# Retention in chunks of 64 tokens: scores and K^T V in quadrants of the array, values and state in one product

## The chip, the cores and the metric

The kernel runs on one core of a Trainium2 chip. The metric is the device time of the program in microseconds; the kernel before takes 776.05 us, the median of 3 runs (775.56 to 776.47). The profiled execution of it has a span of 773.3 us.

In the profile PE is TensorE's matmuls, PEld its weight loads, DVE VectorE, ACT ScalarE, POOL GpSimd, and SP SyncE, which here issues nearly all transfers (SPq is its queue of instructions).

## The reference

Retention for 8 sequences of 576 tokens with 8 heads of 64 dimensions, then a feed-forward block of 4608 tokens, 512 to 768 to 512, whose hidden value is the maximum of three products.

```python
def _attn_ref(q, k, v):                       # each (8, 8, 576, 64)
    scores = scale * np.matmul(q, k.transpose(0, 1, 3, 2))
    gamma = 1.0 - 2.0 ** (-5.0 - np.arange(H))
    rel = pos[:, None] - pos[None, :]
    Dmat = np.where(rel >= 0, gamma[:, None, None] ** rel[None, :, :], 0.0)
    return np.matmul(scores * Dmat[None], v)

def _moe_ref(x, w1, w2, w3, w_out):           # x is (4608, 512)
    h = np.maximum(np.maximum(x @ w1, x @ w2), x @ w3)
    return h @ w_out
```

Because the decay is a power of gamma, retention can be computed by chunks: inside a chunk with masked scores, and for all earlier tokens through a state, the sum of K^T V so far (64x64 for each head). Values are scaled with gamma to a negative power beforehand, outputs with gamma to a positive one afterwards, and the state is multiplied by gamma^128 from one group of 128 tokens to the next.

## The kernel before

All 4608 tokens are cut into 36 groups `g` of 128 tokens (`C = 128`), four to a tile of 512 tokens. A sequence has 4.5 groups, so every second one begins at token 64 of a group. While the feed-forward block of one tile runs, the groups of the next tile are prepared in 12 steps strewn among its products. The parts that matter here (cuts are marked with `...`):

```python
def load_blocks(g, *blocks):                   # q and k in blocks of 32x32, to be transposed by VectorE
    for n, src in (("q", q), ("kx", k)):
        if 0 in blocks:
            raws[n, g] = raw.tile([P, NP, C // 32, 32], FP32, tag=n, name=n + "raw", bufs=2)
        for blk in blocks:
            for a in range(4):
                nc.sync.dma_start(t[32 * a:32 * a + 32, :, blk, :], src[...])   # 4 heads x 32 x 32

def load(g):                                   # blocks of q and k, then k and v as they are
    if g >= BY_PE and ("q", g) not in raws:
        load_blocks(g, *range(C // 32))
    for n, src in ...:
        bufs = 3 if n == "k" else 2
        ...
            nc.sync.dma_start(t[row:row + m], src[b, :, pos:pos + m, :].rearrange("h p d -> p h d"))

def decay_values(g):
    t = vds[g] = vpool.tile([C, H, D], FP32, tag="vd", name="vd")
    nc.gpsimd.tensor_tensor(t[:], raws.pop(("v", g))[:], gk[:]..., op=ALU.mult)

def scores(g):                                 # two heads at a time, 64 rows of the array each
    chore(len(urgent))                         # first whatever was put off
    for p in range(NP):
        for j in range(2):
            r = slice(D * j, D * (j + 1))
            nc.tensor.matmul(s[j][:, p, :], lhsT=kT[r, p, :], rhs=qT[r, p, :], start=True, stop=True)
    for j in range(2):
        soon(partial(nc.vector.tensor_tensor, st[:, j], s[j][:], masks[start_of(g)][:]..., op=ALU.mult))

def state(g):                                  # K^T V
    for h in range(H):
        nc.tensor.matmul(kvs[g][half(h % 2), h // 2, :], lhsT=kr[r:, h, :], rhs=vds[g][r:, h, :], ...)

def values(chunks, new_states=(), later=False):
    chore(len(urgent))
    for m, g in enumerate(chunks):             # scores times values
        for n in range(NP):
            for c in range(2):
                nc.tensor.matmul(o[n % 2][half(c), m, n // 2, :], lhsT=vds[g][:, h, :], rhs=sts[g][:, h % 2, h // 2, :], ...)
    for g in new_states:
        if g not in kvs:
            state(g)                           # also that of the next pair's first group
    for m, g in enumerate(chunks):             # state times queries, added to it
        ...
                nc.tensor.matmul(o[n % 2][half(c), m, n // 2, :old], lhsT=states[g][r, h // 2, :],
                                 rhs=qks[g]["q"][r, h // 2, :old], start=False, stop=True, ...)

for n in range(0, CPT, 2):                     # the 12 steps of a tile: m is 0 or 6
    a, b, m = CPT * t + n, CPT * t + n + 1, 6 * (n // 2)
    at(m, (keep, a), (transposes, b), (decay_values, b))
    at(m, (load, b + 2))
    at(m + 2, (scores, a), (scores, b))
    at(m + 3, (decay_values, a + 2))
    at(m + 4, (values, [a, b], [b, a + 2]), (transposes, a + 2), (load, a + 4))
```

`soon` puts a step into a queue from which the program takes one at a time between products of the feed-forward block. Groups up to 6 are transposed by TensorE, later ones (`g >= BY_PE`) by VectorE in blocks of 32x32. Every fp32 matmul is two passes, and shows as two instructions in the profile.

Of the kernel before, what the change touches and what calls it, by code (L numbers as in the profile page):

```python
# [80 lines left out]
def kernel(  # L81
# [30 lines left out]
    stp = ctx.enter_context(tc.tile_pool(name="stp", bufs=4))  # L112
# [15 lines left out]
    gk = const.tile([C, H], FP32, name="gk")  # L128
    one, top, inf, first = (const.tile([P, 1], FP32, name=n) for n in ("one", "top", "inf", "first"))
    const.tile([P, FILL // 4], FP32, name="fill")  # L130
    gq = const.tile([P, 2, NP // 2, C], FP32, name="gq")
    gs = const.tile([P, NP, D], FP32, name="gs")
# [6 lines left out]
    causal = const.tile([C, C], FP32, name="causal")  # L139
    nc.gpsimd.memset(causal[:], 1.0)  # L140
    nc.gpsimd.affine_select(out=causal[:], in_=causal[:], compare_op=ALU.is_ge, fill=0.0,
                            base=0, channel_multiplier=-1, pattern=[[1, C]])
# [8 lines left out]
    def start_of(g):  # L151
        r = -g * C % S
        return r if r < C else None

    masks = {0: causal, None: causal}
    for r in sorted({start_of(g) for g in range(NG)} - {0, None}):
        m = masks[r] = const.tile([C, C], FP32, name=f"causal{r}")
        nc.gpsimd.tensor_copy(m[:], causal[:])
        nc.gpsimd.memset(m[0:r, r:C], 0.0)


    raws, vds, qks, sts, states, kvs = {}, {}, {}, {}, {}, {}

    def spans(g):

        row = 0
        while row < C:
            b, pos = divmod(g * C + row, S)
            n = min(C - row, S - pos)
            yield row, b, pos, n  # L170
            row += n

# [14 lines left out]
    def load_blocks(g, *blocks):  # L187
        for n, src in (("q", q), ("kx", k)):

            if 0 in blocks:  # L190
                raws[n, g] = raw.tile([P, NP, C // 32, 32], FP32, tag=n, name=n + "raw", bufs=2)
            t = raws[n, g]
            for blk in blocks:
                b, pos = divmod(g * C + 32 * blk, S)
                for a in range(4):
                    nc.sync.dma_start(
                        t[32 * a:32 * a + 32, :, blk, :],
                        src[b, a // 2::2, pos:pos + 32, 32 * (a % 2):32 * (a % 2) + 32].rearrange("p j i -> j p i"))
# [12 lines left out]

    def decay_values(g):
        t = vds[g] = vpool.tile([C, H, D], FP32, tag="vd", name="vd")
        nc.gpsimd.tensor_tensor(t[:], raws.pop(("v", g))[:], gk[:].unsqueeze(2).to_broadcast([C, H, D]),  # L214
                                op=ALU.mult)
# [4 lines left out]
    def transposes(g):  # L220
        both = qks[g] = {}
        if g >= BY_PE:
            for n in ("k", "q"):
                t = both[n] = att.tile([P, NP, C], FP32, tag=n + "T", name=n + "T", bufs=2 if n == "k" else 3)
                soon(partial(nc.vector.transpose, t[:].rearrange("a p c -> a (p c)"),
                             raws.pop(("kx" if n == "k" else n, g))[:].rearrange("a p b i -> a (p b i)")))
            return
        for n, src in (("k", raws["k", g]), ("q", raws.pop(("q", g)))):
            pool, tag = (ps_r, "r") if g >= CPT else (ps_x, "x")
            pt = pool.tile([P, NP, C], FP32, tag=tag, name=n + "t")  # L230
            for p in range(NP):
                nc.tensor.transpose(pt[:, p, :], pair(src, p), ident[:C, :C])
            t = both[n] = att.tile([P, NP, C], FP32, tag=n + "T", name=n + "T", bufs=2 if n == "k" else 3)
            nc.scalar.copy(t[:], pt[:])

    def scores(g):
        chore(len(urgent))
        qT, kT = qks[g]["q"], qks[g]["k"]
        s = [ps_r.tile([C, NP, C], FP32, tag="r", name=f"s{j}") for j in range(2)]
        for p in range(NP):  # L240
            for j in range(2):
                r = slice(D * j, D * (j + 1))
                nc.tensor.matmul(s[j][:, p, :], lhsT=kT[r, p, :], rhs=qT[r, p, :], start=True, stop=True)  # L243
        st = sts[g] = att.tile([C, 2, NP, C], FP32, tag="st", name="st", bufs=2)
        for j in range(2):
            soon(partial(nc.vector.tensor_tensor, st[:, j], s[j][:],
                         masks[start_of(g)][:].unsqueeze(1).to_broadcast([C, NP, C]), op=ALU.mult))

    def begins(g):
        return g + 1 < NG and start_of(g + 1) != 0  # L250

    def half(j):
        return slice(D * j, D * (j + 1))

    def state(g):

        kr = raws["k", g]
        kvs[g] = None
        if begins(g):
            r = start_of(g) or 0  # L260
            kvs[g] = ps_r.tile([P, NP, D], FP32, tag="r", name="kv")
            for h in range(H):
                nc.tensor.matmul(kvs[g][half(h % 2), h // 2, :], lhsT=kr[r:, h, :], rhs=vds[g][r:, h, :],  # L263
                                 start=True, stop=True)

    def keep(g):
        def step(t, kv):
            if start_of(g) is not None:
                nc.vector.tensor_tensor(t[:], kv[:], gs[:], op=ALU.mult)
            else:  # L270
                nc.vector.tensor_tensor(t[:], kv[:], states[g][:], op=ALU.add)  # L271
                nc.gpsimd.tensor_tensor(t[:], t[:], gs[:], op=ALU.mult)  # L272

        if begins(g):
            t = states[g + 1] = stp.tile([P, NP, D], FP32, tag="state", name="state")
            soon(partial(step, t, kvs[g]))
# [7 lines left out]
    def values(chunks, new_states=(), later=False):  # L284

        def before(g):
            return C if start_of(g) is None else start_of(g)

# [3 lines left out]
        o = [pool.tile([P, len(chunks), NP // 2, C], FP32, tag=tag, name="o") for _ in range(2)]  # L294
        for m, g in enumerate(chunks):
            for n in range(NP):
                for c in range(2):
                    h = head(c, n)
                    nc.tensor.matmul(o[n % 2][half(c), m, n // 2, :], lhsT=vds[g][:, h, :],  # L299
                                     rhs=sts[g][:, h % 2, h // 2, :], start=m == 0 and n < 2,  # L300
                                     stop=before(g) == 0, skip_group_check=True)
        for g in new_states:
            if g not in kvs:
                state(g)
        for m, g in enumerate(chunks):
            old = before(g)
            if old > 0:
                for n in range(NP):
                    for c in range(2):
                        h = head(c, n)  # L310
                        r = half(h % 2)
                        nc.tensor.matmul(o[n % 2][half(c), m, n // 2, :old], lhsT=states[g][r, h // 2, :],  # L312
                                         rhs=qks[g]["q"][r, h // 2, :old], start=False, stop=True,
                                         skip_group_check=True)
        finish = partial(output, chunks, o, t, i)
        if later:
            return finish
        finish()
        for g in new_states[:1]:
            if g >= CPT:  # L320
                keep(g)

    def output(chunks, o, t, i):
        if i == 0:
            xT[t] = xpool.tile([P, NDC, NT], FP32, tag="xT", name="xT")
        for b in range(2):
            shape = [P, NP // 2, len(chunks), C]
            soon(partial(
                nc.vector.tensor_tensor,
                xT[t][:, b::2, i * C:(i + len(chunks)) * C].rearrange("p u (m c) -> p u m c", c=C),  # L330
                o[b][:].rearrange("p m u c -> p u m c"), gq[:, b].unsqueeze(2).to_broadcast(shape), op=ALU.mult))
        i += len(chunks) - 1
# [285 lines left out]
    def ffn(t):  # L618

        h = hpool.tile([P, NF, NT], FP32, tag="h", name="h")  # L620
        if t == 0:
            for fp, i in units:
                for fb in (2 * fp, 2 * fp + 1):
                    maximum = up_plain(t, h, fb, i)
                    if CPT not in qks:
# [63 lines left out]
    for g in range(CPT):  # L689
        load(g)  # L690
        if g == 1:
            for j in range(2):
                nc.sync.dma_start(gs[half(j)], state_decay[half(j), :, half(j)])
# [5 lines left out]
    for c in range(2):  # L699
        of_rows = out_decay[:, NP // 2 * c:NP // 2 * (c + 1), :].rearrange("(b p) u c -> p b (u c)", b=2)  # L700
        nc.scalar.dma_start(gq[half(c)].rearrange("p b u c -> p b (u c)"), of_rows)
# [4 lines left out]
    state(0)  # L706
    first_output = values([0], [0], later=True)
    keep(0)
# [4 lines left out]
    state(1)  # L713
    keep(1)
    values([1], [1])
# [4 lines left out]
    state(2)  # L720
    keep(2)
    convert(2)
    values([2], [2])
    convert(2)
    values([3], [3])
    convert(4)
    keep(3)
# [3 lines left out]
    def steps(t):  # L731
# [4 lines left out]
        def at(n, *what):  # L736
            for step, *args in what:
                if step is values:
                    if args[0][0] < NG:
                        todo[n].append(partial(values, args[0], [g for g in args[1] if g < NG]))  # L740
                elif args[0] < NG:
                    todo[n].append(partial(soon, partial(step, *args)) if step is load else partial(step, *args))

        if t == 1:
            a, b, c, d = range(CPT, 2 * CPT)
            at(0, (load, b))
            at(1, (scores, a), (state, a), (keep, a))
# [3 lines left out]
            at(5, (values, [a, b], [b, c]), (load_blocks, d, 3), (load, d))  # L751
# [76 lines left out]
```

## Time and profile before

| what | value |
|---|---|
| time, median of 3 runs | 776.05 us |
| span of the profiled execution | 773.3 us |
| PE busy | 766.8 us (99%) |
| VectorE busy | 564.1 us (73%) |
| ScalarE busy | 325.9 us (42%) |
| GpSimd busy | 102.9 us (13%) |
| scores, L243 | 576 matmuls, 37.7 us busy |
| scores times values, L299 | 576 matmuls, 35.7 us |
| K^T V, L263 | 512 matmuls, 19.2 us |
| state times queries, L312 | 512 matmuls, 18.4 us |
| block loads of q and k | 464 + 464 transfers of 16 KB |

How to read it: "busy" is the time in which at least one instruction of the kind was under way, and matmuls overlap, so these sums say less than the time from the first matmul of a kind to the next one of another kind. The chain of waits follows the work that ended last back to the beginning; its shares say which engine sets the time. A form such as 64\*128 64x128 means 64 rows and 128 columns of the array in use, with 128 columns of the moving operand. Up to about 24.6 us the first four groups are prepared alone; until about 122 us the weights are converted and the first tile is computed plainly; from then on a tile takes about 82 us, and the last tile has no retention beside it.

### The profile page before, as it was taken

Reading aid. Unit: us, or ns where it says so; the run is one execution under the profiler, and the core shown is the slowest. Engines: PE = TensorE matmul, PEld = TensorE weight load, DVE = VectorE, ACT = ScalarE, POOL = GpSimd, SP = SyncE. Lnnn points to the kernel's source line nnn. Section 1 sums busy time; section 2 is a strip of 40 time slices with the busy share of each in tenths; the row PEclk is TensorE's granted clock in tenths of the full one; section 3 lists DMA queues with packets and bytes.
Section 4 is the critical chain, followed back from the end, with each engine's and each line's share of the span. In section 5 each row is a group of like instructions: output and inputs, shape, how many; then the busy total and the mean of one; then the engine's idle time right before and its main releaser. Section 6 shows DMA issues by size and latency. Waiting matters only on the chain.

```text
span 773.3 us, 14511 instructions
## 1 busy us (share of the span) xinstructions
PE 766.8 (99%) x5032; PEld 626.5 (81%) x5032; DVE 564.1 (73%) x1249; ACT 325.9 (42%) x811; POOL 102.9 (13%) x124
## 2 busy tenths in 40 slices
PE   9999999999999999999999999999999999999998
PEld 8545454688888888888888888888888888888887
DVE  3898989799577856784768757876778568845672
ACT  3665631163254415451346234532544054514551
POOL 2210021111110201111111111110112001200000
PEclk9999999999999999999999999999999999999999
DMA  9995544333333332333233333333333323001001
GB/s 225 241 226 131 158 110 103 59 58 58 92 58 58 57 77 62 56 75 67 62 56 58 59 96 58 57 58 96 58 56 59 84 48 74 3 15 42 2 1 55
DMA packets 237083, 59.33 MB, mean 77 GB/s; under 512 B 217937, under 2 KB 235729, under 8 KB 237009
## 3 DMA queue, kind: packets, MB, share of 16 engines
q1 hardware_dynamic: 236432, 58.07, 34.9%
q8 instruction: 39, 0.64, 0.3%
q10 hardware_dynamic: 576, 0.33, 0.1%
q14 instruction: 36, 0.29, 0.1%
HBM read 48.89 MB, written 9.44 MB: 75 GB/s over the span
## 4 chain that ended last, share of the span: by engine, by line
PE 97%; SPq 1%; DVE 1%; DMA 1%; issue 0%; ACT 0%; DVEq 0%
PE a L588 18%; PE b L588 16%; PE dx L428 11%; PE up L611 11%; PE c L588 8%; PE dz L428 5%; PE d L588 5%; PE e L588 5%; PE s L243 4%; PE o L299 4%; PE down L598 3%; PE dy L428 3%; PE o L312 2%; PE kv L263 2%; SPq L210 1%; DMA qraw<-in_q_dram 1%
## 5 line engine op out<-in xcount | busy, mean ns | idle before, releaser
L568 DVE TENSOR_TENSOR part<-part 128x256 f32<-128x256 f32 x460 | 208.7, 462 | 78.2 <-ACT part L573 70.4
L573 ACT COPY part<-b 128x256 f32<-128x256 f32 x230 | 85.6, 372 | 126.0 <-PE b L588 114.6
L573 ACT COPY part<-a 128x256 f32<-128x256 f32 x276 | 102.7, 372 | 84.9 <-PE a L588 72.3
L214 POOL TENSOR_TENSOR vd<-vraw,gk 128x512 f32<-128x512 f32 x36 | 40.3, 1120 | 339.2 <-DMA vraw<-in_v_dram 219.9
L611 PE MATMUL up<-xT,w 128*128 128x512 f32 (+2 forms) x200 | 84.7, 578 | 0.3 <-DVE w L517 0.3
L588 PE MATMUL a<-s,w 128*128 128x256 f32 x276 | 82.3, 380 | 0.0
L588 PE MATMUL b<-s,n 128*128 128x256 f32 x276 | 82.1, 379 | 0.0
L611 PEld LDWEIGHTS up<-xT,w 128*128 128x128 f32 x200 | 36.8, 190 | 42.3 <-issue 39.2
L588 PEld LDWEIGHTS b<-s,n 128*128 128x128 f32 x276 | 52.4, 190 | 7.1
L588 PEld LDWEIGHTS a<-s,w 128*128 128x128 f32 x276 | 52.3, 190 | 7.3 <-issue 0.2
L588 PE MATMUL c<-xT,w 128*128 128x256 f32 x184 | 56.0, 386 | 0.0
L588 PE MATMUL b<-xT,n 128*128 128x256 f32 x184 | 55.4, 382 | 0.0
L588 PE MATMUL d<-s,w 128*128 128x256 f32 x184 | 55.1, 381 | 0.0
L568 DVE TENSOR_TENSOR h<-part 128x256 f32<-128x256 f32 x92 | 42.6, 463 | 6.6
L588 PE MATMUL e<-xT,w 128*128 128x256 f32 x184 | 47.3, 379 | 0.0
L588 PE MATMUL a<-xT,n 128*128 128x256 f32 x184 | 47.2, 379 | 0.0
L428 PE MATMUL dx<-To,H 128*128 128x256 f32 (+1 forms) x204 | 44.9, 370 | 0.0
L435 ACT COPY part<-dx 128x256 f32<-128x256 f32 (+1 forms) x34 | 10.5, 363 | 80.1 <-PE dx L428 77.9
L178 DVE TENSOR_TENSOR xT<-o,gq 128x512 f32<-128x512 f32 x28 | 18.1, 686 | 33.3 <-PE o L312 33.3
L428 PEld LDWEIGHTS dx<-To,H 128*128 128x128 f32 x204 | 36.6, 190 | 5.5 <-issue 1.0
L243 PEld LDWEIGHTS s<-qT,kT 64*128 64x128 f32 x576 | 33.9, 188 | 7.9 <-PE b L588 4.0
L272 POOL TENSOR_TENSOR state<-state,gs 128x256 f32<-128x256 f32 x24 | 18.6, 776 | 162.1 <-DVE state L271 162.1
(104 smaller groups left out, 1299.8 us busy)
## 6 DMA issues: line engine op xcount, KB each, us to landing
bits<-in_moe_w_dram SPq DMA_DIRECT2D x36, 256.0 KB, 5.6
out_dram<-osb SPq DMA_DIRECT2D x35, 256.0 KB, 2.1
kraw<-in_k_dram SPq DMA_DIRECT2D x32, 256.0 KB, 3.0
vraw<-in_v_dram SPq DMA_DIRECT2D x32, 256.0 KB, 3.4
qraw<-in_q_dram SPq DMA_DIRECT2D x464, 16.0 KB, 1.8
kxraw<-in_k_dram SPq DMA_DIRECT2D x464, 16.0 KB, 1.8
bits<-in_moe_w_out_dram SPq DMA_DIRECT2D x6, 512.0 KB, 4.7
qraw<-in_q_dram SPq DMA_DIRECT2D x6, 256.0 KB, 4.1
```

What stands on the lines that cost most here:

```text
L178: (urgent or chores).popleft()()
L214: nc.gpsimd.tensor_tensor(t[:], raws.pop(("v", g))[:], gk[:].unsqueeze(2).to_broadcast([C, H, D]), op=ALU.mult)
L243: nc.tensor.matmul(s[j][:, p, :], lhsT=kT[r, p, :], rhs=qT[r, p, :], start=True, stop=True)
L263: nc.tensor.matmul(kvs[g][half(h % 2), h // 2, :], lhsT=kr[r:, h, :], rhs=vds[g][r:, h, :], start=True, stop=True)
L272: nc.gpsimd.tensor_tensor(t[:], t[:], gs[:], op=ALU.mult)
L299: nc.tensor.matmul(o[n % 2][half(c), m, n // 2, :], lhsT=vds[g][:, h, :], rhs=sts[g][:, h % 2, h // 2, :], start=m == 0 and n < 2, stop=be ...
L428: nc.tensor.matmul(o, lhsT=hS[n](fp)[:, m * P:(m + 1) * P], rhs=late["T"][n][:, fp, cols], start=first and fp == 0 and (m == 0 or last and ...
L568: nc.vector.tensor_tensor(out, a, b, op=op)
L573: nc.scalar.copy(t[:], ps[step[0]][:])
L588: nc.tensor.matmul(ps[chain][:], lhsT=factor(w, fb), rhs=xS[t][x], start=n == 1, stop=ends, skip_group_check=True)
L598: nc.tensor.matmul(b[:], lhsT=h[:, fb, m * P:(m + 1) * P], rhs=w_sb["out", fb], start=(fb == 0), stop=(fb == NF - 1))
L611: nc.tensor.matmul(ps[:, cols], lhsT=w_sb[i, fb][:, dc * P:(dc + 1) * P], rhs=xT[t][:, dc, cols], start=dc == 0 and cols.start == 0, stop= ...
```

## The change

The unit becomes 64 tokens: each group has two chunks `c`. Scores (64x64 for a head) and K^T V of each chunk (contraction over 64 tokens) are laid out so that four matmuls use the four 64x64 quadrants of the array. The masked scores of a chunk and its queries are stacked in one 128-row operand `ms[g, c]`, its values and the state in another, `vas[g, c]`, so that one product over 128 rows gives values plus state times queries. It is meant to take matmul time off TensorE.

For the stacking the halves have to lie in fixed rows: chunk 0 has values in rows 0 to 63 and the state in rows 64 to 127, chunk 1 the reverse. Values and queries of chunk 0 are moved there by transfers within the core (`move_values`, `move_queries`); for groups up to 6 the scaling and the copies out of PSUM are split instead. Masks and additions of the state (`keep`) now write halves. The state of chunk 0 is added without a decay, and that of chunk 1 is multiplied by GpSimd. Block loads take eight heads at a time. The diff, cut to its core:

```diff
@@ load_blocks
-                raws[n, g] = raw.tile([P, NP, C // 32, 32], FP32, tag=n, name=n + "raw", bufs=2)
+                raws[n, g] = raw.tile([P, H, 2, 32], FP32, tag=n, name=n + "raw", bufs=2)
-                for a in range(4):
+                c, e = divmod(blk, 2)
+                for a in range(2):
+                    r = D * (1 - c) + 32 * a
                     nc.sync.dma_start(
-                        t[32 * a:32 * a + 32, :, blk, :], ...
+                        t[r:r + 32, :, e, :],
+                        src[b, :, pos:pos + 32, 32 * a:32 * a + 32].rearrange("h p i -> p h i"))
@@ values, scaled and moved
+        if g >= BY_PE:
+            vas[g, 1] = vpool.tile([P, H, D], FP32, tag="va1", name="va1")
+            scaled(vas[g, 1], slice(0, C))
+            return
+        for c in range(2):
+            scaled(fresh(g, c), half(c))
+
+    def move_values(g):
+        nc.sync.dma_start(fresh(g, 0)[half(0)], vas[g, 1][half(0)])
...
@@ transposes
-            t = both[n] = att.tile([P, NP, C], FP32, tag=n + "T", ...)
-            nc.scalar.copy(t[:], pt[:])
+            copy = nc.vector.tensor_copy if n == "q" and g < CPT else nc.scalar.copy
+            for c in range(2):
+                for j in range(2):
+                    copy(to[c][half(1 - c), j::2, :], pt[half(j), :, half(c)])
+
+    def move_queries(g):
+        def step():
+            m0 = ms[g, 0] = att.tile([P, H, D], FP32, tag="m0", name="m0", bufs=3)
+            nc.sync.dma_start(m0[half(1)], ms[g, 1][half(1)])
+        soon(step)
@@ scores, now with K^T V
-                nc.tensor.matmul(s[j][:, p, :], lhsT=kT[r, p, :], rhs=qT[r, p, :], start=True, stop=True)
+        for h in range(H):
+            for c in range(2):
+                if place(g, c) < S // D - 1:
+                    nc.tensor.matmul(sk[c][half(c), h, :], lhsT=kr[half(c), h, :], rhs=vas[g, c][half(c), h, :], ...)
+            for c in (1, 0):
+                r = half(1 - c)
+                nc.tensor.matmul(sk[1 - c][half(c), h, :], lhsT=kT[r, h, :], rhs=of_q[c][r, h, :], ...)
+
+        def mask(c):
+            nc.vector.tensor_tensor(ms[g, c][half(c)], sk[1 - c][half(c)], causal[half(c)]..., op=ALU.mult)
+
+        def keep(c):
+            to = fresh(g + 1, 0) if c else vas[g, 1]
+            if place(g, c) == 0:
+                nc.scalar.copy(to[half(c)], sk[c][half(c)])
+            else:
+                nc.vector.tensor_tensor(to[half(c)], sk[c][half(c)], vas[g, c][half(1 - c)], op=ALU.add)
+            if c:
+                nc.gpsimd.tensor_tensor(to[half(1)], to[half(1)], gs[half(1)]..., op=ALU.mult)
...
@@ values
+            for m in range(2):
+                for n in range(NP):
+                    for c in range(2):
+                        nc.tensor.matmul(o[half(c), n, half(m)], lhsT=vas[g, m][:, h, :], rhs=ms[g, m][:, h, :], ...)
...
@@ the steps of a tile
-            at(m, (keep, a), (transposes, b), (decay_values, b))
+            at(m, (move_queries, a), (transposes, b), (decay_values, b))
             at(m, (load, b + 2))
+            at(m + 1, (move_values, b), (move_queries, b))
             at(m + 2, (scores, a), (scores, b))
             at(m + 3, (decay_values, a + 2))
-            at(m + 4, (values, [a, b], [b, a + 2]), (transposes, a + 2), (load, a + 4))
+            at(m + 4, (values, a, b), (move_values, a + 2), (transposes, a + 2), (load, a + 4))
```

## The prediction

> **What bounds the kernel now.** I read, in this order, the page's busy times and its chain, the groups of matmuls, the tensor engine's order of time around one pair of groups, and the order of time of the queue that issues transfers (SPq). From the page and the first 24.6 us:
>
> ```profile
> PE   9999999999999999999999999999999999999998
> PEld 8545454688888888888888888888888888888887
> DVE  3898989799577856784768757876778568845672
> PE 97%; SPq 1%; DVE 1%; DMA 1%; issue 0%; ACT 0%; DVEq 0%
> 0.00:24.60 24.60, 20.98 (x288) 18.39 (x288) 11.78 (x26) 8.97 (x14) 7.68 (x16) 1.00 0.97 218
> 24.60:98.40 73.80, 73.79 (x352) 38.33 (x353) 68.44 (x125) 45.33 (x69) 7.45 (x7) 1.00 0.79 188
> ```
>
> PE is the bound: 97% of the chain, no gap after 24.6 us. VectorE (third pair of numbers) has 5 us to spare out of 74 in the stage in which the weights are converted. So a us taken from PE counts whole from 122.6 us on; every new wait of PE counts whole as well, since nothing else hides behind it.
>
> What retention costs on PE, from one pair of groups (start, length, engine, line, tiles; a piece lasts until the next one starts):
>
> ```profile
> 219.74 2.06 PE L243 MATMUL s<-qT,kT 64*128 64x128 f32 x32
> 221.72 0.70 PE L588 MATMUL c<-xT,w 128*128 128x256 f32 x2
> ...
> 273.57 1.97 PE L299 MATMUL o<-st,vd 128*64 128x128 f32 x32
> 275.37 1.10 PE L263 MATMUL kv<-vd,kraw 128*64 128x64 f32 x32
> 276.40 1.10 PE L312 MATMUL o<-qT,state 64*64 64x128 f32 x32
> 277.44 0.91 PE L428 MATMUL dx<-To,H 128*128 128x256 f32 x3
> ```
>
> A pair takes 1.98 (scores) + 1.80 (values) + 1.03 (K^T V) + 1.04 (state times queries) = 5.85 us. Over 122.6:700, where 14 pairs lie, the chain of waits gives the four lines 4.8 + 4.6 + 2.0 + 2.2 = 13.6% of 577.4 us, 78.5 us, or 5.6 a pair: first and last groups of a sequence need less.
>
> Does a quadrant with 64 moving columns cost half of one with 128? The kernel before has such matmuls, for groups in which a sequence begins at token 64:
>
> ```profile
> 66.95 0.90 PE L312 MATMUL o<-qT,state 64*64 64x64 f32 x32
> 67.78 7.13 PE L611 MATMUL up<-xT,w 128*128 128x512 f32 x16
> ```
>
> Half of these 32 move 64 columns, half 128: 0.83 us against the 1.04 of 32 wide ones. With 27.25 ns for a wide one (a 256-column matmul takes 216 ns, 2.59 us for twelve in the chain; half of that, shared by four quadrants, is 27) a fixed 0.16 is left of 1.03, and 0.83 = 0.16 + 16 x 27.25 + 16 x n gives n = 14.6 ns. So narrow quadrants do run four at a time.
>
> The queue that issues transfers (start, length, in order):
>
> ```profile
> 198.37 10.86 SPq L440 DMA_DIRECT2D out_dram<-osb  x4
> 209.32 7.57 SPq L196 DMA_DIRECT2D qraw<-in_q_dram  x16
> 216.94 8.68 SPq L196 DMA_DIRECT2D kxraw<-in_k_dram  x16
> 225.72 0.38 SPq L210 DMA_DIRECT2D kraw<-in_k_dram  x1
> 226.20 0.53 SPq L210 DMA_DIRECT2D vraw<-in_v_dram  x1
> 226.82 7.98 SPq L196 DMA_DIRECT2D qraw<-in_q_dram  x16
> ```
>
> This queue is seldom idle: the load of one group holds it for 17.5 us (209.32 to 226.82), two groups in the 41 us of a pair. A transfer costs it some 0.47 us (7.57/16) whether it has 16 KB or 256 KB (0.38, 0.53). Today that is harmless, because loads run two groups ahead.
>
> **What the Trainium skill says.** "TensorEngine Tiling", Key Properties: tiles load and multiply independently, but a change of tiling mode drains the array. The trace agrees: four quadrants share a 108 ns slot, and about 0.16 us is left over where the mode changes. The same page, PSUM Bottleneck: tiling speeds up TensorE and not the emptying of PSUM. It agrees: masking 128x512 takes VectorE 683 ns before, and 64 rows by 512 columns will, by my estimate, take as long. "DMA: Bandwidth & Descriptors", Anatomy of one DMA: a semaphore wait happens on the issuing sequencer, before dispatch. Our queue fits: the four stores sit on it for 10.86 us until their data is there. "TensorE: Matmul & The Clock Gate", Part 1: after an idle window of about 3.4 us the array runs at half its clock. The first transposes of the trace take 0.85 us for four (4.15 to 5.00), later ones 0.44 (28.18 to 28.62); no idle gap of that length lies later in this trace.
>
> **The change, part by part.**
> Matmuls of a pair. Scores and K^T V: 2 groups (of 128 tokens) x 8 heads x 4 quadrants x 2 passes = 128 x 14.6 ns + 0.16 = 2.03 us. Values with the state stacked: 2 x 8 x 2 x 2 = 64, two column tiles at a time, 29.2 ns each (kv before: 32 in 0.93 of its 1.03) + 0.1 = 1.97. Sum 4.0, 14 pairs 56.0. Saved: 78.5 - 56 = 22.5 us.
>
> VectorE. Of each group the state's addition (409 ns at 128x256) becomes two of 683 ns: about 1 us a group, 3 to 4 us in a tile of 82 us in which it is busy 58 to 60 us. Hidden in the steady part. At the start it isn't: the q copies of four groups move to VectorE as quarters, 16 x about 0.37 = 5.9 us, and 15 masks and additions instead of 8 masks and 3 additions give 10.2 against 6.7 us. Additions now stand ahead of each values product, with GpSimd's factors (two products of 1.04 us instead of one, and 1 us for the state) between them. With four outputs (2.7) and the first weight's conversion (2.9), VectorE's work before the first up product adds up to 21.7 us, from 6.1 us on, with some 3 us of waits: first up at about 30.8 instead of 24.61, +6 us.
>
> While the weights are converted PE would save 3.6 us, but VectorE, at 93%, gets 2.4 us more, and ScalarE copies 8 quarters (372 ns each for 256 columns) instead of 2 halves (590 ns): +1 us net.
>
> Transfers, the part that I think decides. Block loads are halved, 16 a group: 16 x 0.474 + 0.4 + 0.5 + some 0.5 of hiccups = 9.1 us. Two moves a group come in on the same queue, and PE waits for one: K^T V of a group's first half reads values that the queue must first have moved. For the second group of a pair, b, the code puts this move behind the whole load of group b+2. Take the tile that starts at 208.15 us (PE's previous dx ends there). The first scores start at +11.6, those of b at +12.6. On the queue the last store goes at +0.7; behind it stand the load of the group a+2 (9.1), the move of queries (0.5), the load of b+2 (9.1): the move of values goes at about +19.3, and lands some 2.3 us later (16 KB loads land after 1.8, 256 KB after 3.0). PE waits from +12.6 to +21.6: 9 us. In the second pair the queue is free, but the load of b+2 wants a buffer of kraw. There are three, and kraw is now read by the scores of group a, where the kernel before had read it one pair earlier. So: scores of a end, kraw 0.4, vraw 0.5, move 0.5, landing 2.3 with 512 KB ahead of it: about 4 us of PE's time.
>
> Groups 13 and 31 need no moved values for that product (their first half ends a sequence), 35 has no load in front: 6 waits of 9 us (54), 5 of 4 us (20), and for 13 and 31 a VectorE that waits for moved queries, 2 x 3. Each long wait lets the clock fall, an estimate of 1 to 2 us each, 8 in all.
>
> Sum: 776 - 22.5 + 6 + 1 + 54 + 20 + 6 + 8 = 848.5. Because all waits have been taken at full length, I go a little under: 842 us.
>
> **The rivals.**
> First, moves in time: transfers of eight heads take the queue less than 0.2 us each, or PE comes late anyway. Then 776 - 22.5 + 6 + 1 + 2 = about 762. For it: whoever put the moves a step ahead of the scores wanted that, and the number of loads was halved. Against it: no transfer in the lines above costs the queue under 0.38 us, and two loads stand before the move.
> Second, only the kraw wait is real, and the queue gets to the first pair early: 11 waits of 4 us, about 806.
> Third, VectorE becomes the bound in the steady part, as it empties PSUM of four more half tiles a pair: 62 of 78 us speak against it; it would add 5 to 10 us on top of any of these.
> Fourth, quadrants are issue-bound: starts 7 ns apart and 14.6 ns a matmul say no; it would leave the matmuls as long as before, +20.
>
> **Range and chances.** Four fifths of my belief lies with the queue, between the second rival (with shorter waits, 790) and full waits with a slow clock (875). The first rival gets the rest, shared between just over and just under 760.5 us, which is the 2% line. Range 788 to 872; faster 0.08, same 0.14, slower 0.78.
>
> **What would show it.** Quadrants: 128 matmuls of one pair in 2.0 us, net of waits. Waits: PE's waits led by a DMA of the moved values (va0<-va1), about eleven times, long (about 9) and short (about 4) in turn, always between the scores of a and of b; the queue's order of time with that move straight after kraw and vraw. Start: the first up near 30.8 us. Clock: matmuls of 256 columns at more than 216 ns after a long wait. I am wrong if PE is again without gaps after the start, or if the waits sit elsewhere, before the values product, say, on a mask or an addition.

## The result: 931.49 us, and the profile after

The changed kernel takes 931.49 us (median of 4 runs, 929.84 to 934.42) against 776.15 us: a ratio of 1.2006, with an interval of 1.1985 to 1.2027. That is 155 us slower; the prediction had 66 us and a range that ended at 872.

The page of the changed kernel, span 929.1 us: the busy rows in 40 slices, the granted clock in tenths, the chain by engine, and two of its groups and transfers (count, then KB and median us from issue to landing).

```profile
PE   7698999597996697796939697796949994999998
...
DVE  4879998396747666485528566585538763885672
...
PEclk8799999798997899798969899798969997999999
...
PE 62%; SPq 11%; DVE 11%; DMA 8%; issue 6%; ACT 2%; POOL 0%; DVEq 0%; ACTq 0%
...
L277 PE MATMUL sk<-va,kraw 64*64 64x64 f32 x1024 | 52.5, 254 | 118.8 <-DMA va<-va 82.4
...
va<-va SPq DMA_DIRECT2D x29, 128.0 KB, 3.2
```

PE, which before had nines to the end, has a hole about every second slice, and the clock row dips in the same places. The chain has left PE for 38% of the span, most of it for the issuing queue and transfers (SPq 11%, DMA 8%, issue 6%). One group of matmuls has nearly all of the idle time in front of it: K^T V, 118.8 us.

PE's waits of the changed kernel (us in all, times, longest) say the same by releaser:

```profile
PE sk L277 <- DMA va<-va: 82.4, 8, 14.5
PE sk L277 <- issue: 32.1, 3, 12.3
PE d L589 <- DVE part L569: 9.5, 1, 9.5
PE up L612 <- DVE w L518: 9.0, 2, 4.7
PE sk L277 <- POOL va L224: 4.3, 6, 0.8
```

The first two lines are eleven waits, 114.5 us, all before the scores of the second group of a pair. Three of them are put down to "issue", which is time for which the profile shows no cause; but they stand at the same place in the program and end at the same event. Here is one of those three, the pair of groups 16 and 17, with PE first and then the queue's order of time (start, length):

```profile
364.80 0.23 PE L281 MATMUL sk<-m,kT 64*64 64x64 f32 x2
377.00 0.33 PE L277 MATMUL sk<-va,kraw 64*64 64x64 f32 x1 [11.97 <-issue]
```

```profile
352.99 0.37 SPq L441 DMA_DIRECT2D out_dram<-osb  x1
353.45 3.92 SPq L195 DMA_DIRECT2D qraw<-in_q_dram  x8
357.41 3.90 SPq L195 DMA_DIRECT2D kxraw<-in_k_dram  x8
...
362.48 0.94 SPq L264 DMA_DIRECT2D m<-m  x1
363.52 4.01 SPq L195 DMA_DIRECT2D qraw<-in_q_dram  x8
367.58 3.92 SPq L195 DMA_DIRECT2D kxraw<-in_k_dram  x8
...
372.67 0.74 SPq L234 DMA_DIRECT2D va<-va  x1
...
374.15 0.54 SPq L234 DMA_DIRECT2D va<-va  x1
401.66 3.79 SPq L195 DMA_DIRECT2D qraw<-in_q_dram  x8
```

Two whole loads (353.45 and 363.52, nine us each) stand between the last store and the move of values that PE needs. The values themselves have been ready since 339.3, when GpSimd had scaled them. PE is ready for the move at 365.0; the queue issues it at 372.67, it lands at 376.9, and PE goes on at 377.00. The blocks of q and k that make up nearly all of those two loads are first read at 399.0, when VectorE transposes them.

The time from the first matmul to the next of another kind, without gaps, added up for three stretches (my own sums from the starts in each trace; "steady" is from the first product with sums of tiles to the end):

| us | first up product | from there to the steady part | steady: gaps | retention | other products | rest |
|---|---|---|---|---|---|---|
| before | 24.6 | 120.8 | 0 | 76.7 | 548.1 | 3.1 |
| after | 37.8 | 145.4 | 115.9 | 67.0 | 559.6 | 3.4 |
| difference | +13.2 | +24.6 | +115.9 | -9.7 | +11.5 | +0.3 |

The first of the eleven waits (11.5 us, at 173 us) lies in the second column.

### The profile page after: what moved, and what is told of

Its sections match the earlier page's. It is cut to its first block, busy times and chain, and to the rows that moved or that the text cites. A ratio compares the mean times of both kernels' runs of the same rounds, so it can differ in the third digit from the quotient of the medians.

```text
span 929.1 us, 16538 instructions
## 1 busy us (share of the span) xinstructions
PE 777.0 (84%) x6184; PEld 629.4 (68%) x6184; DVE 607.0 (65%) x1285; ACT 337.7 (36%) x845; POOL 131.4 (14%) x146
## 4 chain that ended last, share of the span: by engine, by line
PE 62%; SPq 11%; DVE 11%; DMA 8%; issue 6%; ACT 2%; POOL 0%; DVEq 0%; ACTq 0%
PE a L589 11%; PE b L589 10%; PE dx L429 9%; SPq L195 9%; PE c L589 6%; PE dz L429 4%; PE o L321 4%; PE d L589 4%; DMA va<-va 3%; DVE part L569 3%; PE e L589 3%; PE up L612 3%; PE sk L277 3%; PE down L599 2%; PE dy L429 2%
## 5 line engine op out<-in xcount | busy, mean ns | idle before, releaser
L277 PE MATMUL sk<-va,kraw 64*64 64x64 f32 x1024 | 52.5, 254 | 118.8 <-DMA va<-va 82.4
L277 PEld LDWEIGHTS sk<-va,kraw 64*64 64x64 f32 x1024 | 47.2, 164 | 128.4 <-issue 119.3
L294 DVE TENSOR_TENSOR va<-sk,va 64x512 f32<-64x512 f32 x56 | 38.6, 689 | 92.5 <-PE sk L281 89.0
L612 PE MATMUL up<-xT,w 128*128 128x512 f32 (+2 forms) x200 | 90.7, 611 | 9.1 <-DVE w L518 9.0
L296 POOL TENSOR_TENSOR va<-va,gs 64x512 f32<-64x512 f32 x32 | 35.3, 1107 | 410.1 <-DVE va L294 182.3
L285 DVE TENSOR_TENSOR m<-sk,causal 64x512 f32<-64x512 f32 x72 | 49.5, 687 | 19.9 <-DMA m<-m 15.4
L589 PE MATMUL c<-xT,w 128*128 128x256 f32 x184 | 61.5, 418 | 0.0
L224 POOL TENSOR_TENSOR va<-vraw,gk 128x512 f32<-128x512 f32 (+1 forms) x43 | 48.0, 1117 | 35.5 <-DMA vraw<-in_v_dram 27.2
L281 PE MATMUL sk<-m,kT 64*64 64x64 f32 x1152 | 50.7, 252 | 0.0
L281 PEld LDWEIGHTS sk<-m,kT 64*64 64x64 f32 x1152 | 45.6, 163 | 0.2 <-ACT m L258 0.2
```

The costliest lines, as they stand in the source:

```text
L224: nc.gpsimd.tensor_tensor(t[rows], v_raw[rows], factor, op=ALU.mult)
L277: nc.tensor.matmul(sk[c][half(c), h, :], lhsT=kr[half(c), h, :], rhs=vas[g, c][half(c), h, :], start=True, stop=True)
L281: nc.tensor.matmul(sk[1 - c][half(c), h, :], lhsT=kT[r, h, :], rhs=of_q[c][r, h, :], start=True, stop=True)
L285: nc.vector.tensor_tensor(ms[g, c][half(c)], sk[1 - c][half(c)], causal[half(c)].unsqueeze(1).to_broadcast([D, H, D]), op=ALU.mult)
L294: nc.vector.tensor_tensor(to[half(c)], sk[c][half(c)], vas[g, c][half(1 - c)], op=ALU.add)
L589: nc.tensor.matmul(ps[chain][:], lhsT=factor(w, fb), rhs=xS[t][x], start=n == 1, stop=ends, skip_group_check=True)
```

## The experiments

The theory: the moves wait behind loads on a queue that issues in order, and this makes up most of the loss. The rivals: the buffers of kraw (which I had taken for the cause in every second pair), the transfers themselves (their latency, whatever their place), and an overloaded VectorE. Ratios are to the kernel before, which took 776.4 to 776.7 us beside these runs.

**Moves ahead of the load.** The same transfers on the same queue, but values and queries of group b are moved before the load of b+2.

```diff
-            at(m, (move_queries, a), (transposes, b), (decay_values, b))
+            at(m, (move_queries, a), (transposes, b), (decay_values, b), (move_values, b), (move_queries, b))
             if a == 2 * CPT:
                 at(m, (load, a + 2))
             at(m, (load, b + 2))
-            at(m + 1, (move_values, b), (move_queries, b))
```

> Moves of values and queries of a pair's second group put ahead of the load of the group after next; nothing else. Theory 1 (the transfer queue is in order, and the move stands behind two whole loads): in the first pair of a tile one load is still ahead, so a wait of 0 to 3 us is left there, none in the second pair; the 114 us of PE waits at the scores fall under 25, the 9.5 us wait for VectorE goes, the clock stays up; about 795 us (780 to 815). Theory 2 (the three buffers of kraw decide): the same here, so this run does not tell 1 from 2. Theory 3 (VectorE's larger work of emptying PSUM in halves is what slows the steady part, and PE would wait elsewhere): over 880 us.

Measured: 802.09 us, ratio 1.0322 (1.0305 to 1.0339). This change of order gives back 129 us. PE's waits for moved values that are left:

```profile
PE sk L277 <- DMA va<-va: 8.2, 3, 4.3
...
PE sk L277 <- issue: 4.9, 2, 3.2
```

These are five, of 1.7 to 4.3 us (0 to 3 were expected), each in the first pair of a tile, where one load (of a+2) still stands ahead; second pairs have none. The position on the queue is the cause.

**A fourth buffer of kraw**, in the changed kernel.

```diff
-            bufs = 3 if n == "k" else 2
-            pool, bufs = (raw0, 1) if g < BY_PE and g % (bufs + 1) == bufs else (raw, bufs)
+            bufs = 4 if n == "k" else 2
+            pool, bufs = (raw0, 1) if g < BY_PE and g % (bufs + 1) == bufs and n != "k" else (raw, bufs)
```

> Four buffers for kraw instead of three; order of the queue as in the changed kernel. Theory 1: nothing, 925 to 936 us, as the queue reaches the load of kraw after the scores that free the buffer. Theory 2 (as my prediction had it for the second pair): five or six waits shorter by 4 us or more each, 885 to 910 us.

Measured: 935.86 us, 1.2046 (1.2027 to 1.2065). No gain, and the five waits of the second pairs add up to 37.7 us as against 38.4: that rival falls, and with it my reason for these waits. The trace of the changed kernel shows the true one. First the queue's waits between 352 and 430 us, then what it issued from 409 us on, for the second pair (groups 18 and 19):

```profile
SPq L195 <- DVE part L569: 27.5, 2, 27.2
```

```profile
409.93 0.58 SPq L209 DMA_DIRECT2D vraw<-in_v_dram  x1
410.56 1.08 SPq L264 DMA_DIRECT2D m<-m  x1
411.74 5.12 SPq L195 DMA_DIRECT2D qraw<-in_q_dram  x8
416.89 3.91 SPq L195 DMA_DIRECT2D kxraw<-in_k_dram  x8
...
421.97 1.05 SPq L234 DMA_DIRECT2D va<-va  x1
```

After 374.7 the queue looked free. It was not: at its head stood the load of group a+4, and this waited 27.2 us for a buffer of q, which VectorE empties when it transposes group a+2 (400.93 to 401.63; the load goes at 401.66). So that load and the next one run back to back again just before PE wants the move: scores of a end at 418.5, the move goes at 421.97 and lands at 426.4, PE waits 8.1 us. The load into the buffer of kraw goes at 420.9, 2.4 us after those scores have let it go, so it did not wait for them.

**Moves on another queue.** Both moves are issued by ScalarE's queue; nothing else changes.

```diff
-        nc.sync.dma_start(fresh(g, 0)[half(0)], vas[g, 1][half(0)])
+        nc.scalar.dma_start(fresh(g, 0)[half(0)], vas[g, 1][half(0)])
@@ move_queries
-            nc.sync.dma_start(m0[half(1)], ms[g, 1][half(1)])
+            nc.scalar.dma_start(m0[half(1)], ms[g, 1][half(1)])
```

> Both moves issued from ScalarE's queue, where no load stands before them; their place in the program is unchanged. Theory 1: PE's waits for moved values go (under 15 us of 114), about 795 us. Rival: ScalarE, also in order, waits itself for GpSimd's values and VectorE's transposes, its copies out of PSUM come late, and PE waits for those instead: over 850 us with waits at a and b on ScalarE.

Measured: 787.85 us, 1.0142 (1.0123 to 1.016), 144 us less than the changed kernel. PE's waits with the moves on ScalarE's queue:

```profile
PE up L612 <- DVE w L518: 9.2, 3, 4.7
PE sk L277 <- POOL va L224: 4.8, 6, 1.5
PE d L589 <- DVE part L569: 4.3, 4, 1.1
...
PE down L599 <- DVE h L616: 1.8, 1, 1.8
...
PE down L599 <- DVE w_out L518: 1.4, 1, 1.4
```

No wait for a moved tile is left. The sizes of the moves are the same (128 KB, 29 of each), so their latency costs PE no wait once they start in time. "DMA: Bandwidth & Descriptors" of the Trainium skill, section "Issuing engines are not separate DMA queues", says that issuing from several engines only saves sequencer time, "which is usually small relative to the DMA itself". Here it isn't small: 18 us of sequencer time stand before a transfer that lands 4.2 us after its issue, and the second queue is worth 144 us.

**No transfers at all.** Values are scaled twice by GpSimd, in halves, and ScalarE copies the queries from half to half of the partitions.

```diff
-        if g >= BY_PE:
-            vas[g, 1] = vpool.tile([P, H, D], FP32, tag="va1", name="va1")
-            scaled(vas[g, 1], slice(0, C))
-            return
         for c in range(2):
             scaled(fresh(g, c), half(c))
@@ move_values
-        nc.sync.dma_start(fresh(g, 0)[half(0)], vas[g, 1][half(0)])
...
+        pass
@@ move_queries
-            nc.sync.dma_start(m0[half(1)], ms[g, 1][half(1)])
+            nc.scalar.copy(m0[half(1)], ms[g, 1][half(1)])
```

> No moves by transfer: GpSimd scales each half of the values straight into its place (two products of 64 rows), ScalarE copies the half of the queries. Result the same. Theory 1: all waits at the scores go; 931 less 114 of waits, 9.5 of VectorE's and some 20 of slow clock, about 785 us (770 to 800), and what stays above the kernel before is the start and the stage of conversion. Theory 3: over 880 us.

Measured: 793.6 us, 1.0218 (1.0198 to 1.0238). That is 5.8 us slower than with transfers on the other queue: the transfers as such are not the loss, and work on compute engines in their place costs more. Its largest waits in the steady part are for VectorE (7.0 us at d, in four waits).

**Twice as many loads.** The opposite direction, in the changed kernel: each block load as two, of four heads.

```diff
-                    nc.sync.dma_start(t[r:r + 32, :, e, :], src[b, :, pos:pos + 32, ...])
+                    for hs in (slice(0, H // 2), slice(H // 2, H)):
+                        nc.sync.dma_start(t[r:r + 32, hs, e, :], src[b, hs, pos:pos + 32, ...])
```

> The changed kernel, each block load split into two of four heads: 32 instead of 16 transfers a group, as many bytes. Theory 1 (two loads stand before the move on the issuing queue, some 0.49 us a transfer): each wait that now lasts 12 or 8 us grows by up to 2 x 16 x 0.47 = 15 us, eleven of them and the one through the queries: 1050 to 1120 us. If bytes or DMA engines set the wait, not issue: 931 us as it is.

Measured: 1124.38 us, 1.4477 (1.4456 to 1.4498). PE's waits with twice as many loads:

```profile
PE sk L278 <- DMA va<-va: 193.5, 8, 29.0
PE sk L278 <- issue: 82.2, 4, 27.3
```

The bytes are the same and the transfers half as large, but each load now holds the queue for about 16 us instead of 8, and the eleven waits of before grow by 13 to 15 us each. Two loads with 16 more transfers each at 0.47 us are 15. What holds up the issue of the move is the number of transfers ahead of it, not their bytes.

**PE kept busy in the waits.** To see what the slow clock costs apart from the waits: 54 or 36 matmuls of 128x128, whose results are overwritten, ahead of the scores of the eleven waiting groups.

```diff
+        if 9 <= g < 35 and g % 2 and g not in (13, 31):
+            for _ in range(54 if g % 4 == 1 else 36):
+                nc.tensor.matmul(sk[0][:, 0:2, :]..., lhsT=ident[:], rhs=ident[:], start=True, stop=True)
```

> The changed kernel, and in eleven of the waits dummy matmuls of 128x128 on TensorE (54, 11.7 us, in a tile's first pair, 36, 7.8 us, in its second), overwritten by the scores: the waits stay as long, but the array isn't idle. If the clock that falls to half after a long wait costs time of its own: 12 to 25 us less than the 931.5 of the changed kernel, 907 to 920 us, and hardly a window at half clock after 170 us. If not: 930 us or more.

Measured: 925.11 us, 1.1907 (1.1872 to 1.1941). The time at half clock in the steady part fell from 123 us to 24 us, the other products from 559.6 to 554.0 us; the kernel gained only 6.4 us, less than the 12 to 25 expected. In three of the eleven groups the added matmuls outlast the landing of the move, by 0.4 to 0.6 us, 1.4 us in all; so on top of some 115 us of waits the slow clock behind them cost about 6 to 8 us.

**The start.** Three attempts, all with the moves on ScalarE's queue. In the first, VectorE copies q for group 0 alone, instead of four groups (ScalarE does the others). In the second the output factors gq come in two transfers instead of four.

```diff
-            copy = nc.vector.tensor_copy if n == "q" and g < CPT else nc.scalar.copy
+            copy = nc.vector.tensor_copy if n == "q" and g < 1 else nc.scalar.copy
```

> Moves on ScalarE's queue as in e3_moves_on_act (787.85 us), and at the start the copies of the queries of groups 1 to 3 out of PSUM by ScalarE instead of VectorE (12 of 16 copies, 1.75 us of VectorE a group). If VectorE sets the start: 5.25 us less of its work, first up 3 to 5 us earlier than 37.1 us, about 783.5 us. If the latency from GpSimd's scaling through additions to values sets it: first up unchanged within 1 us or later, as ScalarE then makes 8 copies in a row (3 us), about 788 us.

```diff
-        for b in range(2):
-            nc.scalar.dma_start(gq[half(c), b::2, :], out_decay[half(b), NP // 2 * c:NP // 2 * (c + 1), :])
+        of_rows = out_decay[:, NP // 2 * c:NP // 2 * (c + 1), :].rearrange("(b p) u c -> p b (u c)", b=2)
+        nc.scalar.dma_start(gq[half(c)].rearrange("p b u c -> p b (u c)"), of_rows)
```

> As e3_moves_on_act (787.85 us, first up at 37.1 us), gq in two transfers. If ScalarE's queue holds up the start there too: first up 2 to 4 us earlier, about 785 us; if VectorE's work sets the start, as my prediction had it: less than 1 us.

Measured: 787.7 us, 1.0138 (1.0114 to 1.0161), with the first up at 36.0 instead of 37.1; and 788.12 us, 1.015 (1.0135 to 1.0164), with it at 36.8. Neither alone sets the start. In the third, groups 0 to 8 are computed as before the change, and only groups from 9 on in chunks of 64 (of the diff, the conditions alone).

```diff
+    NEW = 9
@@ load_blocks, decay_values, move_values, transposes, scores, values
-        if g >= BY_PE:
+        if g >= NEW:      # as in the changed kernel, moves on nc.scalar
+        if g < NEW:       # as in the kernel before
```

> Groups 0 to 8 (the start, the stage of conversion, and the whole first two sequences) computed as in the kernel before, groups 9 to 35 as in e3_moves_on_act. If the start and the conversion are all that e3 loses: the kernel before until its first product of sums at 145.4 us, then e3's 616.7 us in place of 627.9: about 763 us (757 to 768), and faster than both kernels. If the quadrants bring nothing net in the steady part, 775 us or more.

Measured: 772.17 us, 0.9942 (0.9921 to 0.9963): first up at 29.2, and 123.0 us from there to the steady part instead of 130.6. That is 9 us more than expected: the start stayed 4.6 us behind the kernel before, the stretch to the steady part 2.2, and the steady part took 1.6 us more than with all groups changed. Together with gq in two transfers:

> As e7_new_from_group_9 (772.17 us, first up at 29.2 us), with the output factors gq loaded in two transfers as in the kernel before, not in four. ScalarE issues them, and in e7 it sat 4.3 us behind them with the first copies out of PSUM waiting. If that is what e7 still loses at the start: first up at 25 to 26 us, about 768.5 us. If the start is set by the loads of q and k: no change, 772 us.

Measured: 771.01 us, 0.9929 (0.9916 to 0.9941, 5 runs), with the first up at 27.5: faster than both kernels, by 0.7% and by 17%. The two ratios overlap, so what the two transfers bring is not shown by the time. Two rows of the page of this version, and its first waits of PE:

```profile
PE   7899999999999999999999999999999999999998
...
PEclk9999999999999999999999999999999999999999
```

```profile
PE qt L282 <- DMA qraw<-in_q_dram: 2.9, 5, 0.7
PE d L718 <- DVE part L698: 2.1, 2, 1.1
PE kt L282 <- DMA kraw<-in_k_dram: 2.0, 2, 1.2
```

PE is full again after the start. But of the 21.3 us that retention saves in its steady part (76.7 to 55.4) only 9.7 arrive: gaps take 6.8 and the other products 4.7.

**Less work for VectorE.** To see whether VectorE takes the rest: in the 771.01 us version, one of the two masks of a group and one of its two additions are done for one head instead of eight. This leaves out part of the computation; its time only tells what that work costs.

```diff
+            hs = slice(0, 1 if c else H)
-            nc.vector.tensor_tensor(ms[g, c][half(c)], sk[1 - c][half(c)], causal[half(c)]..., op=ALU.mult)
+            nc.vector.tensor_tensor(ms[g, c][half(c), hs], sk[1 - c][half(c), hs], causal[half(c)]..., op=ALU.mult)
@@ keep
+                hs = slice(0, H if c else 1)
-                nc.vector.tensor_tensor(to[half(c)], sk[c][half(c)], vas[g, c][half(1 - c)], op=ALU.add)
+                nc.vector.tensor_tensor(to[half(c), hs], sk[c][half(c), hs], vas[g, c][half(1 - c), hs], op=ALU.add)
```

> As e8_gq_two_loads, with part of VectorE's work left out (output not the reference's): for groups from 9 on the mask of the second half and the addition of the first half's state are done for one head instead of eight, some 0.6 us less for each of about 52 instructions, 31 us in all. If VectorE, late with joins and masks, gives back half of what the quadrants save in the steady part (22 us saved on retention's matmuls, 9.5 left in e7): 5 to 11 us less than e8. If the loss is TensorE's own (mode changes, weight loads): the same as e8 within 2 us.

Measured: 766.0 us, 0.9868 (0.9843 to 0.9892), 5 us less; gaps in the steady part 1.4 us instead of 6.8. The mask goes from 0.68 to 0.23 us and the addition from 0.69 to 0.22, some 22 us of VectorE in all (31 were expected), 0.8 us a group. That is about as much as the change had added: an addition of 0.41 us became two of 0.69. So VectorE accounts for a little under half of the 11.5 us that were missing. The other products still take 551.7 us against 548.1; these 3.6 us stay open.

## Why the prediction was right in kind and too small in size

The direction, the mechanism and the place of the waits were as predicted. Two steps of the working on transfers failed. The move was to land 2.3 us after its issue, but the eleven moves that PE waited for landed after 3.1 to 4.5 us, 43.6 us in all instead of 25.3. And in the second pairs the queue was not free: two loads stood ahead there too. The eleven waits came to 114.6 us instead of 74. Going below the sum, to 842 us, because the waits had been taken at full length, went the wrong way. The terms of the sum, one by one:

| term of the prediction | predicted | measured | from |
|---|---|---|---|
| matmuls of 14 pairs | -22.5 | -22.0 | steady retention, 76.7 to 54.7, moves on the other queue |
| start, first up | +6 | +13.2 | 24.6 to 37.8 |
| conversion stage | +1 | +9.8 | 120.8 to 130.6, moves on the other queue |
| six waits in first pairs | +54 | +76.2 | 11.5, 12.0, 14.5, 12.0, 13.9, 12.3 |
| five waits in second pairs | +20 | +38.4 | 6.8, 7.9, 8.1, 7.9, 7.7 |
| groups 13 and 31 | +6 | +9.5 | one wait, group 13 |
| clock | +8 | +6 to +23 | see below |

With 23 us for the clock these terms leave 8 of the 155.8 us between the two profiled runs: 4.6 of other products that stay longer with the moves on the other queue (552.7 to 548.1), and 3.6 of small gaps and rest.

**Quadrants.** Right: four narrow matmuls share the array at the cost worked out from 16 of them in the kernel before. With the moves on the other queue, scores and K^T V of a pair take 2.02 to 2.06 us; 2.03 were predicted. The rival of quadrants bound by issue is refuted by the -22.0.

**First pairs.** The right wait at the right place, mis-sized: 12.7 us on average instead of 9. I took 2.3 us for the move to land, between the times of loads of 16 and of 256 KB. Of the 13 moves that had no load in flight ahead of them, 11 did land in 2.2 to 2.4 us. But the eleven that PE waited for had such loads in flight. At 372.67 the move had 512 KB of kraw and vraw just ahead of it, which landed at 374.95 and 376.40, and it took 4.2. The rest of the error in this wait: PE arrives 7.6 us before the issue instead of 6.7, and half of the difference is the move of queries, 0.94 us on the queue instead of 0.5. In the two longest waits, 14.5 and 13.9 us, one of the loads ahead is of a group that belongs to two sequences: its kraw and vraw take two transfers each, 2.7 us of the queue instead of 0.9.

**Second pairs.** This step failed. "In the second pair the queue is free" was read from the number of transfers, not from what the head of the queue waits for. The head was a load that waited 27.2 us for VectorE, so two loads again stood ahead: 7.7 us on average instead of 4. In the pair of groups 18 and 19 the move went 3.5 us after the scores of a instead of 1.4, and landed 4.5 us later instead of 2.3. The kraw buffer, named as cause, had no part in it, as the run with a fourth buffer shows.

**Groups 13 and 31.** As said, no wait for moved values; in group 13 PE waited through VectorE for moved queries. VectorE's order of time shows the mask of that group held up:

```profile
278.23 0.69 DVE L285 TENSOR_TENSOR m<-sk,causal 64x512 f32<-64x512 f32 x1 [10.08 <-DMA m<-m]
```

The additions behind it on VectorE are late by as much, and PE waits 9.5 us at d. Near group 31 PE's longest wait is 2.0 us, for a sum of VectorE. So this term was one wait and not two.

**Start.** Mis-sized: 13.2 us instead of 6. From 6.1 us to the first up VectorE is busy for 23.8 us against the 21.7 predicted (2.0 of the difference are waits for GpSimd, see the last section), but it is idle for 7.9 us, and I had allowed 3. Its first 22 us in the changed kernel:

```profile
6.63 1.75 DVE L258 COPY m<-qt 64x256 f32<-64x256 f32 x4 [5.63 <-PE qt L254]
10.57 0.68 DVE L285 TENSOR_TENSOR m<-sk,causal 64x512 f32<-64x512 f32 x1 [2.19 <-PE sk L281]
12.30 0.69 DVE L294 TENSOR_TENSOR va<-sk,va 64x512 f32<-64x512 f32 x1 [1.05 <-ACT va L292]
...
13.75 1.75 DVE L258 COPY m<-qt 64x256 f32<-64x256 f32 x4
18.39 0.68 DVE L294 TENSOR_TENSOR va<-sk,va 64x512 f32<-64x512 f32 x1 [2.89 <-PE sk L281]
```

Copies, scores, mask, addition and factor of each group wait for one another across PE, VectorE, ScalarE and GpSimd; the three longest idle times, 2.2, 1.1 and 2.9 us, are in these lines. A sum of one engine's work misses such a chain. Moving three groups' copies away brought only 1.1 us, so VectorE is not alone in it; computing the first nine groups as before brought 7.9. Which link is longest stays open. The 771.01 us version, with the old scheme there, starts at 27.5 and not 24.6; up to then its PE waits 3.5 us for loads of q and k (0.5 in the kernel before), which is about the difference. Why these loads come later stays open.

**Conversion stage.** Mis-sized: +9.8 without the queue's waits. The engine that I had noted at 93% was given more, and I charged 1 us net. With the moves on the other queue PE waits 7.7 us for VectorE there: 4.3 us for its conversion of weights (at 77 us), 1.4 for that of w_out, 1.8 for a maximum, and 0.2. The up products take 4.6 us longer, for part of which the array is at half clock (3.4 us from 76.6 on). Against that stand 3.1 us saved on retention, where I had 3.6.

**Clock.** Predicted 8 us. Filled waits gave 6.4, at most about 8. On the other side, from the changed kernel to the one with moves on the other queue, retention itself goes from 67.0 to 54.7 us, the other products from 559.6 to 552.7, and the conversion stage, without its wait, from 133.9 to 130.6: 22.5 us. Some of this is not the clock, and part of it may cost nothing, where PE only waits the shorter for the next move; the runs do not tell these apart. In the pair of groups 18 and 19 the 64 matmuls of a start within 0.94 us; the 64 of b, behind the wait, within 1.80, with the clock at half from 422.9 to 429.8.

Of the rivals, "only the kraw wait is real" and "in time" are refuted by the trace. VectorE as the bound was no rival to the waits, but is part of what is left in the steady part when they are gone: 5 us, the lower end of what I gave it.

## What to carry to other kernels

A queue that issues in order makes every transfer wait for those in front and for what they wait for: before adding a small transfer that an engine needs, list what stands ahead of it at that moment, count the transfers for the time of its issue and the bytes just ahead for that of its landing (here 4.2 us instead of 2.2), and look at the buffer that the head of the queue waits for; a queue that looks idle may be blocked. Put such a transfer ahead of the prefetches, or on a queue of its own. And when matmul time is bought with more work for VectorE and GpSimd, try changing over only once the pipeline is full: at the start that work lay bare here, 13.2 us of it.

## What the runs showed of the hardware

VectorE is slowed by GpSimd, but only in some instructions. At the start of the changed kernel, VectorE and then GpSimd (start, length):

```profile
31.68 0.69 DVE L285 TENSOR_TENSOR m<-sk,causal 64x512 f32<-64x512 f32 x1
32.41 0.74 DVE L496 TENSOR_SCALAR expo<-bits 128x512 int32<-128x512 int32 x1
33.07 1.26 DVE L501 TENSOR_SCALAR frac<-bits 128x512 int32<-128x512 int32 x1
...
34.97 1.49 DVE L507 SCALAR_TENSOR_TENSOR mant<-frac,mant 128x512 f32<-128x512 int32 x1
...
38.30 0.42 DVE L496 TENSOR_SCALAR expo<-bits 128x512 int32<-128x512 int32 x1
38.63 0.42 DVE L501 TENSOR_SCALAR frac<-bits 128x512 int32<-128x512 int32 x1
39.16 0.69 DVE L507 SCALAR_TENSOR_TENSOR mant<-frac,mant 128x512 f32<-128x512 int32 x1
```

```profile
31.82 1.04 POOL L296 TENSOR_TENSOR va<-va,gs 64x512 f32<-64x512 f32 x1 [2.33 <-PE o L321]
32.94 1.11 POOL L224 TENSOR_TENSOR va<-vraw,gk 64x512 f32<-64x512 f32 x1
...
34.87 1.04 POOL L224 TENSOR_TENSOR va<-vraw,gk 64x512 f32<-64x512 f32 x1
```

The conversion steps that start beside a GpSimd product take 0.74, 1.26 and 1.49 us, and 0.42, 0.42 and 0.69 alone; they end 0.3 to 0.6 us after GpSimd does. The same holds over the whole trace of the changed kernel. The additions part<-part, with both inputs in SBUF, take 0.42 us (median) away from GpSimd's products, and 0.83 (median) in the 53 cases in which they start during one. The masks, with one of their two inputs in PSUM, take 0.68 us (median) away from them and 0.69 to 0.70 in all ten cases in which they start during one. That agrees with "SBUF — State Buffer" of the Trainium skill, section "Who interferes with whom", by which a VectorE instruction with two SBUF inputs contends with a GpSimd instruction that reads SBUF, as does one in a mode that uses a second port, and whichever of the two engines comes first keeps the shared ports for its whole instruction, while a VectorE instruction with a single SBUF input outside such modes doesn't contend. (That the steps with one input, L496 and L501, run in such a mode is not shown here.)

The change raises GpSimd's busy time from 102.9 to 131.4 us, and such waits are a cost of it that I had not put into the sum. At the start they make 2.0 us in the three steps above, just before the first up product waits for the converted weight: nearly all of what VectorE was busy beyond the prediction. (The kernel before lost 0.7 us of this kind in its first conversion.) How much of the whole loss they make was not measured.
